# Two gated layers behind an attention: part of a weight combination moved to a later batch, first weights loaded before the stage that reads them, left sides made four steps ahead, a conversion paced later

## The chip, the cores and the metric

One core of a Trainium2 chip runs the whole kernel. The metric is the device time in microseconds (us); lower is better. Five instruction streams run side by side and wait for each other through semaphores: PE (matrix products), DVE (vector), ACT (scalar and activation functions), POOL (a second vector engine), and SP, which in this kernel does nothing but issue DMA transfers, in the order in which its rows stand.

## The reference, cut to what matters

```python
def _attn_ref(q, k, v, tau):                      # 4 x 8 heads, 576 x 64
    scores = scale * np.matmul(q, k.transpose(0, 1, 3, 2))
    thresh = np.max(scores, axis=-1, keepdims=True) - tau
    scores = np.where(scores >= thresh, scores, -1000000000.0)
    ...
    return np.matmul(attn, v)

def _moe_ref(x, w_in, w_out, s, b):               # 2304 x 512 -> 2048 -> 512
    r = np.maximum(x @ w_in, 0.0)
    return (s * (r * r) + b) @ w_out

def _moe2_ref(x, w_in, w_out):                    # 2304 x 512 -> 2048 -> 512
    h = x @ w_in
    g = h * np.tanh(np.log1p(np.exp(np.minimum(h, 20.0))))   # sp = h where h > 20
    return g @ w_out

def reference(...):
    x = attention, heads side by side, (2304, 512)
    return _moe2_ref(_moe_ref(x, ...), ...)
```

The weights of both layers arrive as pairs of 32-bit words (64-bit numbers), and are turned into 32-bit floats on the chip.

## The kernel before, in words

Each factor of a product is held as a high and a low part, and three matmuls stand for one product: high by high, high by low, low by high.

**Stages.** Attention runs over 16 pairs of heads, four to a batch. `moe1(b)` is the first layer for batch b; its steps (128 of them per batch) are run between the steps of the attention for batches 0, 1 and 2, and batch 3 runs alone, once the attention is over. `split_w` (L45 to L70) turns the first layer's weights into floats and splits them; it is paced by a counter `k` in `run` (L737 to L742) and by the steps of batch 0. Then `moe2` (L699) runs the second layer in three superbatches `sb` of 768 tokens. In each, `hidden(sb, j)` for j = 0 to 7 makes the hidden values, and `output(sb)` multiplies them by the output weights.

**Seven products in place of eight.** The second layer multiplies 2 x 2 blocks with seven products, numbered p = 1 to 7, whose left and right sides are sums and differences of blocks. The right sides of the weights are made by `combine` (L72): for k = "i" (input weights) and "o" (output weights) and j = 0 to 7, that is 16 blocks. A block is a generator of 14 steps: two loads of raw words (`craw`, L85); six steps that turn them into floats `af` (ACT L92, DVE L93, L95, L97); two with sums and differences `cs` on DVE (L101 to L117); four that split (`chl`: ACT L123, POOL L124) and store to DRAM (`wsi`, `wso`, L126). Before the change all 16 run during `moe1(1)` and `moe1(2)`, at 240 steps over the 256 steps of these two batches, with buffers of a pool `pre2` (two `raw`, two `hl2`, one `af`).

**Left sides.** For the hidden values they come from `y_combos` (L520), which reads the first layer's output `yd` back and makes `yc` 1 to 7 (ACT L539, DVE L540). For superbatch 0 that happens within `moe1(3)`; for the next superbatch it runs within `hidden`, its results go to DRAM (`ycd`), and `output` loads them as `yc` after each p (L696). For the output, `left(p, q)` (L621) gives block q of the left side of product p, with DVE operations (`z`, `s`, `g`), and a copy on ACT (L685) and a subtraction on DVE (L686, which all stand under L619, the helper `tt`) make it into `hl`, in a pool of 8 buffers.

**Weights of `hidden` and `output`.** Each `hidden` loads its seven right sides in two transfers (`wi`, L578) into the pool `wr`; each half of a p in `output` loads one (`wo`, L682).

**What sets the order.** The order of the code, as each engine's own stream: an instruction waits for its operands and buffers, and all behind it on the same engine waits with it. On ACT three copies of finished p = 1 sums (`after`, L661) are written after the last matmul of p = 1, ahead of the casts for p = 6. In `moe1(3)` a weight unit `w3` (L452, 5 buffers, 32 units) is loaded just before the products that use it; SP holds it back until a buffer is free.

Of the kernel before, what the change touches and what calls it, by code (L numbers as in the profile page):

```python
# [8 lines left out]
F32 = mybir.dt.float32  # L9
# [6 lines left out]
P = 128  # L16
# [3 lines left out]
class Fused:  # L20
# [51 lines left out]
    def combine(self, k, j, pool):  # L72
# [3 lines left out]
        af = pool.tile([P, 4, 2, 128], I32, tag="af", name=f"af{k}{j}", bufs=1)  # L76
        raws = []
        for h in range(2):
            raw = pool.tile([P, 512, 2], I32, tag="raw", name=f"craw{k}{j}{h}")
# [20 lines left out]
        s = pool.tile([P, 4, 2, 128], F32, tag="raw", name=f"cs{k}{j}")  # L100
# [28 lines left out]
    def combine_all(self, pool):  # L129
        for k in "io":  # L130
            for j in range(8):
                yield from self.combine(k, j, pool)
# [440 lines left out]
    def hidden(self, sb, j):  # L573
        nc = self.nc
        w = {}
        for ps, o in (((6, 5, 1), 0), ((2, 4, 7, 3), 3)):
            t = self.wr.tile([P, len(ps), 2, 2, 128], F32R, tag="w", name=f"wi{sb}_{j}_{o}")
            nc.sync.dma_start(t.bitcast(F32).rearrange("p q h c n -> p q h (c n)"), self.ws["i"][:, j, o:o + len(ps)])  # L578
            for i, p in enumerate(ps):
                w[p] = t[:, i]  # L580
        if j % 2 == 0:
# [33 lines left out]
    def output(self, sb):  # L615
        nc = self.nc
        nt = N2 // 128
        z, bank, held = {}, {}, {}
# [56 lines left out]
        for p in (1, 6, 2, 7, 5, 4, 3):  # L675
            old = {2: 1, 7: 6, 3: 5}.get(p)
            bank[p] = bank[old] if old else [self.ps.tile([P, 512], F32, tag="ps", name=f"o{p}{sb}_{t}")[:, :256] for t in range(nt)]
            pos = (6, 5, 7, 4, 1, 2, 3).index(p)
            for q in range(4):
# [15 lines left out]
            if sb < 2:
# [13 lines left out]
    def run(self, ctx):  # L709
# [104 lines left out]
N2 = 384  # L814
# [48 lines left out]
```

## Time and profile before

| | us |
|---|---|
| median of 3 runs | 1189.35 (1185.48 to 1190.13) |
| the profiled execution, its own time | 1189.16 |
| its span (first to last instruction) | 1187.4 |
| PE busy in the span | 1110.4 (94%) |
| DVE, ACT, POOL busy | 761.3, 614.5, 424.0 |
| attention with `moe1(0)` to `moe1(2)` | 0 to about 709 |
| `moe1(3)` alone | 709 to 809.5 |
| superbatch 0: hidden, output | 816.7 to 877.4, 877.4 to 941.2 |
| superbatch 1: hidden, output | 941.2 to 999.4, 999.4 to 1061.3 |
| superbatch 2: hidden, output | 1061.3 to about 1119, to 1183.7 |

A trace row gives the instant at which an instruction began and how long it took, and in brackets how long its engine had been idle before it and which instruction let it go on. A row with a count (x6) is a run of equal instructions. Of matmuls, the distance from one start to the next is the pace; the durations overlap. The granted clock of PE stands in tenths or as a share of full speed, 1.00 being 2.4 GHz and 0.50 being 1.2 GHz.

### The profile page before, as it was taken

The numbers are of one execution on the slowest core, as the hardware profiler recorded it, in microseconds if no ns is written. First come the engines' busy times: TensorE is split into PE (matmuls) and PEld (weight loads), VectorE is DVE, ScalarE is ACT, GpSimd is POOL, SyncE is SP. The second block draws the span as 40 slices with busy tenths as digits, with TensorE's granted clock in tenths as the row PEclk, the third lists the DMA queues.
The fourth block names the chain that finished last, engine by engine and source line by source line (L and its number), as shares of the span: only waits on it lengthen the run. The fifth ranks groups of instructions, "written<-read, shape, count | busy, mean of one in ns | idle before, by whom it ended". The sixth has DMA issues, their size and how long they took to land.

```text
span 1187.4 us, 21376 instructions
## 1 busy us (share of the span) xinstructions
PE 1110.4 (94%) x7896; PEld 1019.3 (86%) x7896; DVE 761.3 (64%) x1515; ACT 614.5 (52%) x1153; POOL 424.0 (36%) x536
## 2 busy tenths in 40 slices
PE   5798999998999999999999989997999999999988
PEld 4576777878898888878888879997999999999988
DVE  5788667777766677776766715322688367825583
ACT  4566666655576655667646537432354134513351
POOL 4666656565666646559656520000000000000000
PEclk7699999999999999999999999998999999999999
DMA  8844466675788788798877668546999999987764
GB/s 214 257 102 119 107 201 198 219 227 174 221 270 267 231 293 247 259 279 258 269 231 268 216 198 286 160 142 229 346 397 383 298 347 385 412 280 248 265 229 129
DMA packets 141447, 292.69 MB, mean 247 GB/s; under 512 B 52832, under 2 KB 78944, under 8 KB 132896
## 3 DMA queue, kind: packets, MB, share of 16 engines
q1 hardware_dynamic: 134112, 286.91, 73.2%
q10 hardware_dynamic: 7232, 4.43, 1.4%
q8 instruction: 62, 1.02, 0.4%
q14 instruction: 41, 0.34, 0.1%
HBM read 201.85 MB, written 66.58 MB: 226 GB/s over the span
## 4 chain that ended last, share of the span: by engine, by line
PE 51%; DMA 16%; DVE 11%; POOL 8%; ACT 6%; issue 6%; SPq 2%; ACTq 0%; POOLq 0%; DVEq 0%
PE o L691 14%; PE y L460 8%; PE h L460 7%; PE qY L571 6%; PE qX L571 4%; PE qV L571 4%; PE pv L365 3%; DMA wraw<-in_moe_w_in_dram 2%; DMA crawi<-in_moe_w_in_dram 2%; DVE e L321 2%; POOL e L331 2%; PE S L306 2%; PE T L343 2%; DMA wsi<-chli 2%; POOL chlo L124 2%
## 5 line engine op out<-in xcount | busy, mean ns | idle before, releaser
L691 PE MATMUL o<-wo,hl 128*128 128x256 f32 x1512 | 182.9, 283 | 7.5 <-ACT hl L685 5.5
L691 PEld LDWEIGHTS o<-wo,hl 128*128 128x128 f32 x1512 | 181.2, 191 | 9.1 <-ACT hl L685 6.3
L460 PE MATMUL h<-xh,w 128*128 128x288 f32 x768 | 165.2, 299 | 5.0 <-ACT r L481 3.7
L460 PE MATMUL y<-gh,w 128*128 128x288 f32 x768 | 168.2, 303 | 1.4 <-ACT y L505 0.9
L321 DVE SCALAR_TENSOR_TENSOR e<-ns,st,e 128x576 f32<-128x576 f32 x128 | 127.4, 999 | 50.8 <-POOL st L312 27.8
L331 POOL TENSOR_SCALAR e<-e,st 128x576 f32<-128x576 f32 x128 | 133.2, 1049 | 38.9 <-DVE st L326 36.9
L460 PEld LDWEIGHTS y<-gh,w 128*128 128x128 f32 x768 | 127.3, 190 | 13.2 <-issue 8.3
L460 PEld LDWEIGHTS h<-xh,w 128*128 128x128 f32 x768 | 125.9, 188 | 9.6 <-ACT r L481 4.8
L317 ACT ACTIVATE e<-ns,st 128x576 f32<-128x576 f32 x128 | 98.9, 776 | 57.9 <-DVE ns L310 55.1
L310 DVE TENSOR_SCALAR_CACHE_REDUCE ns<-S 128x576 f32<-128x576 f32 x144 | 107.5, 749 | 22.1 <-PE S L306 21.0
L343 PE MATMUL T<-ident,e 128*128 128x128 f32 x576 | 98.9, 281 | 21.1 <-ACT te L354 13.6
L306 PE MATMUL S<-KH,Q 128*128 128x288 f32 x320 | 101.5, 333 | 15.4 <-DVE ns L310 9.0
L460 PE MATMUL y<-gl,w 128*128 128x288 f32 x384 | 114.3, 299 | 0.0
L460 PE MATMUL h<-xl,w 128*128 128x288 f32 x384 | 113.3, 295 | 0.0
L354 ACT COPY te<-T 128x576 f32<-128x576 f32 x144 | 91.0, 632 | 41.4 <-PE T L348 35.1
L312 POOL TENSOR_SCALAR st<-st,small 128x1 f32<-128x1 f32 x144 | 66.3, 461 | 119.6 <-DVE ns L310 97.2
L365 PE MATMUL pv<-te,rawv 128*64 128x288 f32 x640 | 98.3, 419 | 0.0
L343 PEld LDWEIGHTS T<-ident,e 128*128 128x128 f32 x576 | 71.2, 143 | 31.2 <-ACT te L354 16.2
L484 POOL TENSOR_TENSOR gl<-rr,gh 128x288 fp32r<-128x288 f32 x96 | 87.9, 922 | 27.0 <-ACT rr L483 26.9
L306 PE MATMUL S<-KL,Q 128*128 128x288 f32 x320 | 93.3, 307 | 0.0
L306 PEld LDWEIGHTS S<-KH,Q 128*128 128x128 f32 x320 | 63.9, 200 | 30.1 <-DVE ns L310 14.8
L571 PE MATMUL qY<-yc,wi 128*128 128x384 f32 x432 | 86.7, 339 | 0.0
(142 smaller groups left out, 2268.0 us busy)
## 6 DMA issues: line engine op xcount, KB each, us to landing
w<-w SPq DMA_DIRECT2D x96, 512.0 KB, 4.6
wo<-wso SPq DMA_DIRECT2D x42, 1024.0 KB, 8.4
wi<-wsi SPq DMA_DIRECT2D x24, 1024.0 KB, 6.9
wi<-wsi SPq DMA_DIRECT2D x24, 768.0 KB, 5.4
w<-wp SPq DMA_DIRECT2D x32, 512.0 KB, 3.7
wsi<-chli SPq DMA_DIRECT2D x24, 512.0 KB, 4.0
wso<-chlo SPq DMA_DIRECT2D x24, 512.0 KB, 3.6
ycd<-yp SPq DMA_DIRECT2D x14, 768.0 KB, 7.3
```

The costliest lines, as they stand in the source:

```text
L306: nc.tensor.matmul(so, Q[:, c0:c0 + 128], kt[:, ks], start=(i == 0), stop=(i == len(terms) - 1))
L310: nc.vector.tensor_scalar(ns.rearrange("p (h n) -> p h n", h=2), sv, -0.125, 3.0e38, op0=ALU.mult, op1=ALU.min, accum_out=nm[:, c1])
L317: nc.scalar.activation(e, ns, AF.Exp, bias=nm[:, c1], scale=-1.0)
L321: nc.vector.scalar_tensor_tensor(e, ns, nthr[:, c1], e, op0=ALU.is_le, op1=ALU.mult, accum_out=sm[:, c1])
L331: nc.gpsimd.tensor_scalar(t, t, rinv[:, j:j + 1], u[:, j:j + 1], op0=ALU.mult, op1=ALU.add)
L343: nc.tensor.transpose(T[:, i * 128:i * 128 + 128], self.es[pr, i, "pair"][:, o:o + 128], self.ident)
L354: nc.scalar.copy(te, T[:, :576])
L365: return self.nc.tensor.matmul(self.pv[HALVES[h], hf * HB:hf * HB + 288], v[:, h, c, :], tes[h][:, hf * 288:hf * 288 + 288], start=first, ...
L460: nc.tensor.matmul(acc[:, :n], w[:, wl, c], rhs[c][xl][:, ts], start=(i == 0), stop=(i == 11))
L484: (nc.vector if b == 3 else nc.gpsimd).tensor_tensor(gl[:, ts], r2, gh[:, ts].bitcast(F32), op=ALU.subtract)
L571: self.nc.tensor.matmul(acc, a, b, start=(first and i == 0), stop=(i == n - 1), skip_group_check=True)
L691: nc.tensor.matmul(bank[p][t], hl[:, gl, j, ts], w[:, 2 * (q % 2) + j, wl], start=(old is None and q + j + i == 0), stop=(q + j + i == 6), ...
```

## The change: five edits

- **Combination.** `EARLY` = 154 steps, 11 blocks (all of "i", and j = 0 to 2 of "o"), are run in `moe1(1)` and `moe1(2)`, spread over all 256 steps; the other 5 blocks ("o", j = 3 to 7, 70 steps) run in `moe1(3)`, one step for each of its first 80 steps, in the buffers of the pool `hl`.
- **Left sides of superbatch 0.** `y_combos(0)` gets its first step at step 80 of `moe1(3)`, then every fourth (before: every eighth from step 0).
- **First weights.** The seven right sides of `hidden(0, 0)` are loaded into three `hl` buffers before `moe1(3)` is finished; `hidden` takes them as an argument.
- **Left sides of the output** are made four (p, q) steps ahead: `prep(0)`, `prep(1)`, `prep(2)` after j = 2, 4, 6 of `hidden`, `prep(3)` at its end, and `prep(i + 4)` at step i.
- **Conversion.** The first layer's weight conversion starts at `k` > 48 and then takes a step for every 12 (before: for every 24, from 24).

```diff
-    def combine(self, k, j, pool):
+    def combine(self, k, j):
+        pool, tags = self.home
-        af = pool.tile([P, 4, 2, 128], I32, tag="af", name=f"af{k}{j}", bufs=1)
+        af = pool.tile([P, 4, 2, 128], I32, tag=tags[0], name=f"af{k}{j}", **tags[3])
...
-    def hidden(self, sb, j):
-        w = {}
-        for ps, o in (((6, 5, 1), 0), ((2, 4, 7, 3), 3)):
-            t = self.wr.tile([P, len(ps), 2, 2, 128], F32R, tag="w", name=f"wi{sb}_{j}_{o}")
-            nc.sync.dma_start(t.bitcast(F32).rearrange("p q h c n -> p q h (c n)"), self.ws["i"][:, j, o:o + len(ps)])
+    def weights_in(self, sb, j, pool, tag, parts):
+        w, o = {}, 0
+        for ps in parts:
+            t = pool.tile([P, len(ps), 2, 2, 128], F32R, tag=tag, name=f"wi{sb}_{j}_{o}")
+            self.nc.sync.dma_start(t.bitcast(F32).rearrange("p q h c n -> p q h (c n)"), self.ws["i"][:, j, o:o + len(ps)])
             for i, p in enumerate(ps):
                 w[p] = t[:, i]
+            o += len(ps)
+        return w
+
+    def hidden(self, sb, j, w):
...
+        seq = [(p, q) for p in (1, 6, 2, 7, 5, 4, 3) for q in range(4)]
+        def prep(i):
+            if i >= len(seq):
+                return
+            p, q = seq[i]
+            a = left(p, q)
+            hl = ready[i] = self.hl.tile([P, 2, 2, N2], F32R, tag="hl", name=f"hl{sb}_{p}_{q}")
+            nc.scalar.copy(hl[:, 0], a)
+            tt(hl[:, 1], a, hl[:, 0].bitcast(F32))
+
+        def run():
+            for i, (p, q) in enumerate(seq):
+                prep(i + 4)
...
-                a = left(p, q)
-                hl = self.hl.tile([P, 2, 2, N2], F32R, tag="hl", name=f"hl{sb}_{p}_{q}")
-                nc.scalar.copy(hl[:, 0], a)
-                tt(hl[:, 1], a, hl[:, 0].bitcast(F32))
+                hl = ready.pop(i)
...
+    def moe2(self, w):
         for sb in range(3):
             nxt = self.y_combos(sb + 1, False) if sb < 2 else iter(())
+            prep, run = self.output(sb)
             for j in range(8):
-                self.hidden(sb, j)
-                next(nxt, None)
+                w = w or self.weights_in(sb, j, self.wr, "w", ((6, 5, 1), (2, 4, 7, 3)))
+                self.hidden(sb, j, w)
+                w = None
+                for _ in range(2 if j == 0 else 1):
+                    next(nxt, None)
+                if j in (2, 4, 6):
+                    prep(j // 2 - 1)
             drain(nxt)
-            self.output(sb)
+            prep(3)
+            run()
...
-            if k % 24 == 0:
+            if k > 48 and k % 12 == 0:
                 next(w1)
...
-                    while n * 256 < 240 * (i + 128 * (b - 1)):
+                    while n * 256 < EARLY * (i + 128 * (b - 1)):
                         next(comb, None)
                         n += 1
                     yield c
-            drain(comb)
+            for _ in range(EARLY - n):
+                next(comb, None)
...
+        self.home = self.hl, ("hl", "hl", "hl", {})
         first = self.y_combos(0, True)
         for i, c in enumerate(self.moe1(3)):
-            if i % 8 == 0:
+            if i < 80:
+                next(comb, None)
+            elif i % 4 == 0:
                 next(first, None)
+        drain(comb)
         drain(first)
+        w0 = self.weights_in(0, 0, self.hl, "hl", ((6, 5, 1), (2, 4, 7), (3,)))
...
+EARLY = 14 * 11
```

A scheduler orders each stream, so the rows below show what the edits moved. Names end in a number of the buffer's own; `hl0_6_1` is superbatch 0, p = 6, q = 1.

ACT at the change from hidden to output in superbatch 0, before (`g` are hidden values, `p1` the copies of finished p = 1 sums):

```order
L613 ACTIVATE g0_3_10281<-g0_3_10281 128x768
L610 ACTIVATE g0_3_10281<-g0_3_10281 128x384
L613 ACTIVATE g0_3_10281<-g0_3_10281 128x768
L661 COPY p10_10497<-o10_0_10412 128x256
L661 COPY p10_10497<-o10_1_10413 128x256
L661 COPY p10_10497<-o10_2_10414 128x256
L685 CAST hl0_6_0_10518<-s0_0_10516 128x768
L685 CAST hl0_6_1_10543<-s0_1_10541 128x768
```

The same place after:

```order
L688 CAST hl0_6_0_10430<-s0_0_10428 128x768
L688 CAST hl0_6_1_10460<-s0_1_10458 128x768
L618 ACTIVATE g0_3_10294<-g0_3_10294 128x768
L688 CAST hl0_6_2_10485<-s0_2_10483 128x768
L615 ACTIVATE g0_3_10294<-g0_3_10294 128x384
L618 ACTIVATE g0_3_10294<-g0_3_10294 128x768
L666 COPY p10_10527<-o10_0_10433 128x256
L666 COPY p10_10527<-o10_1_10434 128x256
L666 COPY p10_10527<-o10_2_10435 128x256
L688 CAST hl0_6_3_10512<-s0_3_10510 128x768
L688 CAST hl0_2_0_10539<-g0_0_9877 128x768
```

The first three casts for p = 6 now stand ahead of the three copies, which wait for PE; they stood behind them. Superbatches 1 and 2 read alike.

SP at the end of `moe1(3)`, before (`yd` are stores of the first layer's output, `wi` the input weights of the second):

```order
L514 DMA yd3_0_63<-yo3_0_9751 128x576
L514 DMA yd3_0_63<-yo3_1_9784 128x576
L514 DMA yd3_1_64<-yo3_2_9817 128x576
L514 DMA yd3_1_64<-yo3_3_9850 128x576
L578 DMA wi0_0_0_9871<-wsi_65 128x1536
L578 DMA wi0_0_3_9873<-wsi_65 128x2048
L578 DMA wi0_1_0_9939<-wsi_65 128x1536
L578 DMA wi0_1_3_9941<-wsi_65 128x2048
```

And after:

```order
L578 DMA wi0_0_0_9853<-wsi_65 128x1536
L578 DMA wi0_0_3_9855<-wsi_65 128x1536
L453 DMA w3_1_3_0_9721<-w1_1_3_0_3682 128x1024
L578 DMA wi0_0_6_9857<-wsi_65 128x512
L453 DMA w3_1_3_1_9754<-w1_1_3_1_3770 128x1024
...
L515 DMA yd3_0_63<-yo3_0_9751 128x576
L544 DMA ycd1_1_9944<-yp1_1_9941 128x1536
L515 DMA yd3_0_63<-yo3_1_9784 128x576
L515 DMA yd3_1_64<-yo3_2_9817 128x576
L515 DMA yd3_1_64<-yo3_3_9850 128x576
L578 DMA wi0_1_0_9946<-wsi_65 128x1536
L578 DMA wi0_1_3_9948<-wsi_65 128x2048
```

The weights of j = 0 went ahead of the last four `w3` units; behind the four stores now stand those of j = 1.

SP in the first part of `moe1(3)`, before:

```order
L452 DMA w3_1_0_1_8955<-w1_1_0_1_2034 128x1024
L452 DMA w3_1_0_2_8985<-w1_1_0_2_2130 128x1024
L543 DMA ycd1_1_10003<-yp1_1_10000 128x1536
L452 DMA w3_1_0_3_9018<-w1_1_0_3_2215 128x1024
L452 DMA w3_0_1_2_9048<-w1_0_1_2_2284 128x1024
L452 DMA w3_0_1_3_9095<-w1_0_1_3_2351 128x1024
L452 DMA w3_0_2_0_9137<-w1_0_2_0_2435 128x1024
```

And after (`craw` are raw words loaded for the combination, `chl` its split results, stored to `wso`):

```order
L453 DMA w3_1_0_1_8834<-w1_1_0_1_1950 128x1024
L86 DMA crawo40_8675<-in_moe2_w_out_dram 128x1024
L86 DMA crawo41_8689<-in_moe2_w_out_dram 128x1024
L453 DMA w3_1_0_2_8872<-w1_1_0_2_2046 128x1024
L127 DMA wso_66<-chlo30_8616 128x2x512
L127 DMA wso_66<-chlo32_8632 128x2x512
L127 DMA wso_66<-chlo34_8647 128x512
L453 DMA w3_1_0_3_8907<-w1_1_0_3_2142 128x1024
L127 DMA wso_66<-chlo35_8663 128x2x512
L453 DMA w3_0_1_2_8950<-w1_0_1_2_2227 128x1024
L453 DMA w3_0_1_3_9005<-w1_0_1_3_2296 128x1024
L86 DMA crawo50_8844<-in_moe2_w_out_dram 128x1024
```

Between the `w3` loads there are now raw loads and stores of split results; up to three stores stand in a row.

## Rows read from the trace of the kernel before

**Rows 1.** Windows: length, busy us of PE, PEld, DVE, ACT, POOL, clock, DMA share, GB/s.
```profile
368.00:709.00 341.00, 325.32 (x2375) 286.50 (x2373) 230.72 (x496) 201.00 (x403) 201.61 (x227) 0.99 0.79 251
709.00:809.50 100.50, 99.98 (x750) 99.52 (x750) 37.15 (x68) 48.03 (x116) 0.00 (x0) 1.00 0.57 190
809.50:941.20 131.70, 122.38 (x842) 121.81 (x842) 78.45 (x114) 49.52 (x75) 0.00 (x0) 0.95 0.91 343
```

**Rows 2.** Timeline of PE where the second layer begins: start, length, instructions, idle before.
```profile
809.21 0.30 PE L460 MATMUL y<-gh,w 128*128 128x288 f32 x1
816.68 2.26 PE L571 MATMUL qX<-yc,wi 128*128 128x384 f32 x6 [7.18 <-DMA wi<-wsi]
...
822.31 1.20 PE L571 MATMUL qX<-yc,wi 128*128 128x384 f32 x6
823.35 0.86 PE L571 MATMUL qY<-yc,wi 128*128 128x384 f32 x4
```

**Rows 3.** Windows, as Rows 1, of the first products there.
```profile
817.00:821.00 4.00, 4.00 (x14) 4.00 (x14) 0.03 (x1) 1.76 (x2) 0.00 (x0) 0.50 1.01 426
```

**Rows 4.** SP's issues there, and the landing times of the five `wi` issues of 811.4 to 813.5.
```profile
811.37 2.65 SPq L578 DMA_DIRECT2D wi<-wsi  x5
...
DMA to landing us min/median/max: 5.2/8.6/12.8
```

**Rows 5.** Windows of L691 alone (PE, PEld): the three outputs, 30 us of full pace.
```profile
877.43:941.18 63.75, 61.61 (x504) 60.96 (x504) 0.97 0.95 352
999.43:1061.25 61.82, 59.60 (x504) 58.97 (x504) 1.00 0.96 365
1114.30:1183.74 69.44, 61.38 (x504) 60.72 (x504) 0.98 0.59 199
...
1020.00:1050.00 30.00, 30.00 (x259) 30.00 (x259) 1.00 0.96 362
```

**Rows 6.** Timeline of PE at the step from p = 1 to p = 6, superbatches 0 and 2.
```profile
887.52 0.97 PE L691 MATMUL o<-wo,hl 128*128 128x256 f32 x6 [1.19 <-ACT hl L685]
889.37 10.86 PE L691 MATMUL o<-wo,hl 128*128 128x256 f32 x77 [0.88 <-DVE hl L619]
...
1132.22 8.01 PE L691 MATMUL o<-wo,hl 128*128 128x256 f32 x53 [1.97 <-ACT hl L685]
```

**Rows 7.** Timeline of ACT, then of DVE, at that step in superbatch 0.
```profile
885.67 1.07 ACT L661 COPY p<-o 128x256 f32<-128x256 f32 x3 [5.14 <-PE o L691]
886.64 3.03 ACT L685 CAST hl<-s 128x768 fp32r<-128x768 f32 x4
...
888.37 0.95 DVE L619 TENSOR_TENSOR hl<-s,hl 128x768 fp32r<-128x768 f32 x1
```

**Rows 8.** Windows, as Rows 1: 45 us of superbatch 0, 10 us of superbatch 1.
```profile
860.00:905.00 45.00, 42.86 (x299) 42.26 (x298) 39.26 (x54) 23.34 (x35) 0.00 (x0) 0.96 1.00 405
...
1010.00:1020.00 10.00, 9.12 (x78) 8.92 (x78) 10.00 (x13) 7.65 (x11) 0.00 (x0) 1.00 1.02 421
```

**Rows 9.** One issue on SP, of the first weights for p = 2, and its time to landing.
```profile
L682 SPq DMA_DIRECT2D wo<-wso x1: 319/319/319, 879.5 to 879.5; - x1
...
DMA to landing us min/median/max: 17.5/17.5/17.5
```

**Rows 10.** Windows, 368 to 709 us, of tile afo (DVE, ACT, POOL), then chlo (ACT, POOL).
```profile
368.00:709.00 341.00, 49.17 (x80) 8.24 (x16) 16.66 (x16) 0.99 0.79 251
...
368.00:709.00 341.00, 17.94 (x32) 38.16 (x32) 0.99 0.79 251
```

**Rows 11.** Waits in 368 to 709 us: who waited for what, total us, times, longest.
```profile
SPq L126 <- POOL chlo L124: 44.6, 20, 5.2
```

**Rows 12.** L95 there: duration ns, min/median/max.
```profile
L95 DVE SCALAR_TENSOR_TENSOR afo<-crawo,afo x16: 675/682/1356, 512.1 to 677.6; 128x512 int32<-128x512 int32 x16
L95 DVE SCALAR_TENSOR_TENSOR afi<-crawi,afi x11: 675/1112/1667, 372.2 to 494.3; 128x512 int32<-128x512 int32 x11
```

**Rows 13.** The page's part 6, DMA issues: count, KB each, median us to landing.
```profile
w<-w SPq DMA_DIRECT2D x96, 512.0 KB, 4.6
```

More of the change, by code (lines that the diff above doesn't have):

```diff
@@ L127, in combine, with combine_all @@
             yield
-    def combine_all(self, pool):
+    def combine_all(self):
         for k in "io":
             for j in range(8):
-                yield from self.combine(k, j, pool)
+                yield from self.combine(k, j)
     def split_all(self, pieces, pool, tags, **kw):
@@ L617, in output @@
         nt = N2 // 128
-        z, bank, held = {}, {}, {}
+        z, bank, held, ready = {}, {}, {}, {}
         tt = lambda o, a, b, op=ALU.subtract: nc.vector.tensor_tensor(o, a, b, op=op)
@@ L673, in after @@
                 store(0, 1, t, add("u2"))
[L675 to L679, printed above, removed]
+        seq = [(p, q) for p in (1, 6, 2, 7, 5, 4, 3) for q in range(4)]
[10 more added lines that the diff above has]
+                prep(i + 4)
+                old = {2: 1, 7: 6, 3: 5}.get(p)
+                if q == 0:
+                    bank[p] = bank[old] if old else [self.ps.tile([P, 512], F32, tag="ps", name=f"o{p}{sb}_{t}")[:, :256] for t in range(nt)]
+                pos = (6, 5, 7, 4, 1, 2, 3).index(p)
                 if q % 2 == 0:
@@ L689, in output @@
                         ts = slice(t * 128, t * 128 + 128)
-                        for i, (gl, wl) in enumerate(((0, 0), (0, 1), (1, 0))):
+                        for k, (gl, wl) in enumerate(((0, 0), (0, 1), (1, 0))):
                             nc.tensor.matmul(bank[p][t], hl[:, gl, j, ts], w[:, 2 * (q % 2) + j, wl],
-                                             start=(old is None and q + j + i == 0), stop=(q + j + i == 6), skip_group_check=True)
+                                             start=(old is None and q + j + k == 0), stop=(q + j + k == 6), skip_group_check=True)
                         if q + j == 4:
                             after(p, t)
-            if sb < 2:
-                t = self.yc[p] = self.ycp.tile([P, 2, 2, N2], F32R, tag=f"yc{p}", name=f"yc{sb + 1}_{p}")
-                nc.sync.dma_start(t.bitcast(F32), self.ycd[p])
-    def moe2(self):
+                if sb < 2 and q == 3:
+                    t = self.yc[p] = self.ycp.tile([P, 2, 2, N2], F32R, tag=f"yc{p}", name=f"yc{sb + 1}_{p}")
+                    nc.sync.dma_start(t.bitcast(F32), self.ycd[p])
+        return prep, run
+    def moe2(self, w):
         for sb in range(3):
             nxt = self.y_combos(sb + 1, False) if sb < 2 else iter(())
+            prep, run = self.output(sb)
             for j in range(8):
-                self.hidden(sb, j)
-                next(nxt, None)
+                w = w or self.weights_in(sb, j, self.wr, "w", ((6, 5, 1), (2, 4, 7, 3)))
[5 more added lines that the diff above has]
+                    prep(j // 2 - 1)
             drain(nxt)
-            self.output(sb)
+            prep(3)
+            run()
     def run(self, ctx):
@@ L758, in moes @@
             pre.close()
-            comb = self.combine_all(pool(a, "pre2", 2, side="left"))
+            self.home = pool(a, "pre2", 2, side="left"), ("af", "raw", "hl2", dict(bufs=1))
             n = 0
```

11 lines of the change are left out of this document (6 added, 5 removed).

## The prediction, made before the change was run

> **What bounds the kernel now.** I read the page's first two parts first: PE is busy 94% of the span, and its slices lie under nine tenths at the start and at a few places near the end. So the time is PE's work plus the holes in it, and the change, which adds and removes no matmul, can only fill holes. The windows by stage say how large they are. From 368 to 709 us PE is idle 341.0 − 325.3 = 15.7 us; in the fourth batch 0.5 us; in superbatch 0 it is 9.3 us [rows 1]. Then I looked for the row on PE that follows each hole, and for what that row waited for. There are two kinds of them in the second layer, and the change aims at both.
>
> The first hole stands between the layers. The last product of the fourth batch starts at 809.21 and the first `qX` at 816.68, after 7.18 us of waiting for `wi` [rows 2]; SP issued it at 811.37, and the first of five landed 5.2 us later [rows 4]. In the 4 us behind it the granted clock is 0.50, so the lower level [rows 3]: PE had stood still, and the first three groups of six, which take 3 × 1.04 = 3.12 us at the pace of 822.31 to 823.35, take 822.31 − 816.68 = 5.63 [rows 2].
>
> The second kind stands in each output, at the step from p = 1 to p = 6. Pace: 30 us / 259 = 0.1158 us for a matmul, 504 of them 58.4 us. The outputs took 63.75, 61.82 and 69.44 us; in the last window 30 matmuls of `hidden` lie too (30 × 1.04/6 = 5.2). The losses are 5.35, 3.4 and 5.84 us, together 14.6 [rows 5]. At that step PE waits for the cast `hl` on ACT, then for its second half on DVE [rows 6], because ACT stood 5.14 us at the three copies, which wait for the end of p = 1, and only then made the four casts from `s`; on DVE the halves then stand between the updates of `g` [rows 7].
>
> **The change, part by part.** The sum is made against the profiled execution, 1189.16 us (its span of 1187.4 and 1.8 around it); the median of the three runs is 1189.35, so the two are one number here.
>
> *A, the first weights.* The hole costs from where the next matmul could have started (809.35, one pace of the fourth batch behind 809.21) to 822.31, less the 3.12 us of work: 9.84 us [rows 2]. In the order of after the three loads of j = 0 stand around the first of the last four `w3`, so they have some four units' time, 12 us, and more to land; the slowest of five queued ones took 12.8 [rows 4]. What is late next is j = 1: its loads still stand behind the four `yd` stores, so 811.4 stays their issue. By the first landing they are there at 816.6; a `hidden` lasts 42 × 1.04/6 = 7.3 us, so PE wants them at 809.4 + 7.3 = 816.7, and the second transfer, with the median 8.6 at 820, half through it. That is just in time. I take 9.3. At the upper end 9.8. At the lower end the first transfer too takes 8.6: 820.0 − 816.7 = 3.3 less, 6.0.
>
> *B, left sides ahead.* In after, the casts for p = 6 stand ahead of the three copies, and so do the DVE halves; nothing in the rows of PE is then late from ACT or DVE. What is late next is DMA. Around that step the 16 engines are full: 405 GB/s over 45 us of superbatch 0, 421 in superbatch 1, shares of 1.00 and 1.02 [rows 8]. The first weights for p = 2 were issued at 879.5, 2.1 us into the output, and landed 17.5 us later, at 897.0 [rows 9]. Without the stall p = 2 begins 144 matmuls into the output: 877.4 + 16.7 = 894.1. So 2.9 us of the 5.35 come back as a wait for `wo`; gain 2.45. In superbatch 1 the stream is at least as full, and in after one more load of `yc` (0.79 MB, 1.9 us at 421 GB/s) stands ahead of the same weights: of 3.4 I leave 0.5. Superbatch 2 loads no `yc` and moves 199 GB/s [rows 5]: 5.84 less two late operations of 0.15, 5.5. Sum 8.5; bounds 5.5 (superbatch 2 alone) and 14.6.
>
> *C, five blocks fewer beside the attention.* The last 14 blocks lay in 368 to 709 us; 9 stay. A block costs DVE 49.17 / 8 = 6.1 us and POOL 38.16 / 8 = 4.8 [rows 10], so the stage loses 31 us of DVE's 231 and 24 of POOL's 202 [rows 1]. PE's time there is set by the chains of the attention through DVE, POOL and ACT, which queue behind the blocks. Whatever share of the 15.7 us of idle is due to the blocks, 5/14 of it goes at most if it is in proportion: 5.6, which I take. Bounds: all 15.7 if the queueing vanishes with less load; and −2, if the attention only meets the batch's steps in another rhythm (two waits of a microsecond).
>
> *M, the same five in the fourth batch.* There PE is idle 0.5 us, so nothing is to be won and everything lies beside it: DVE goes from 37 to 68 us of 100, POOL from 0 to 24 [rows 1, 10]. DMA had 190 GB/s over 100.5 us, 19.1 MB; to it come 5 × (1.05 in and 1.84 out) and the 1.84 of the first weights, 35.4 MB, 352 GB/s, under the 421 that the queues have moved [rows 1, 8]. The cover is the ring of five `w3` buffers: a unit is used up every 100.5/32 = 3.1 us, four units ahead are 12.5 us, a load takes 4.6 [rows 13], so SP may stand about 8 us before PE starves. In after, SP holds up to three stores in a row that each wait for a POOL result; such a wait was 44.6/20 = 2.2 us on the mean [rows 11], 6.7 for three. It fits, but not by much: I take 1.5 us of loss. Bounds: 0, and 5 × 1.2 = 6, one short wait of PE like that in rows 6 for every block.
>
> *Conversion.* The order on every engine is the same as before up to matmul 2064, at about 368 us, and then differs by the combination; so the conversion's other pacing moves nothing: 0, with no range of its own. Moving `y_combos(0)` to the end of the fourth batch costs nothing while DVE is at 68%.
>
> Sum: 1189.2 − 9.3 − 8.5 − 5.6 + 1.5 = **1167.3 us**.
>
> One rule speaks against M. In the stage before, the vector operations of a combination are at times long: L95 has a median of 682 ns in the "o" blocks and 1112 in the "i" blocks, where 675 is the shortest of both [rows 12]. The Trainium skill, "SBUF — State Buffer", section "Who interferes with whom", says that DVE and GpSimd share a port pair as an exclusive lock, and that a DVE instruction with two SBUF inputs contends with a GpSimd instruction that reads SBUF, the loser being fully blocked. By the "i" rows it bites, by the "o" rows, the kind that is moved, it rarely does.
>
> **Rivals.** *R1, DMA does not come late.* For it: the first layer's last loads have taken 1.84 MB out of superbatch 0, 4.4 us of its stream. Against: A puts PE 9.3 us ahead. Then B gives 14: 1189.2 − 9.3 − 14 − 5.6 + 1.5 = 1161.8, and 1152 if C is 15.7. *R2, the attention gives nothing back*, if its chains through DVE, ACT and POOL are set by their own lengths and the blocks only fill gaps; a POOL of 202 us and a DVE of 231 in 341 leave gaps enough [rows 1]: 1189.2 − 9.3 − 8.5 + 1.5 = 1172.9, and 1176.2 with A at 6.0. *R3, DVE becomes the bound of the fourth batch.* If each POOL operation of a block held DVE for its whole length, the first 80 steps (62 us) would hold 23 us of old DVE work, 31 of the blocks and 24 of blocking, 78 us, so PE waits up to 16: 1189.2 − 23.4 + 16 = 1181.8. For it speaks the median of the "i" rows, against it that of the "o" rows [rows 12]. (The Trainium skill's rule above, at its full, is this rival.) *R4, slower: SP's order starves the fourth batch.* Each run of three stores in front of a `w3` load holds it 3 × 5.2 = 15.6 us, the longest wait of rows 11, against a cover of 8: 7.6 us for each block, 38 in five, 1189.2 − 23.4 + 38 = 1204. It decides from 23.4/5 + 8 = 12.7 us for a run. For it: SP takes its rows in order, and DVE and ACT, which feed the blocks, follow PE there. Against: the mean wait is 2.2, and POOL has nothing else to do. That the change doesn't do what it says holds for the conversion, at no price.
>
> **How the numbers follow.** A measurement of this kernel can tell about 0.5% from no change, 5.9 us. The forecast has 0.5, R1 0.2, R2 0.2, R3 0.06, R4 0.04. The range takes in the forecast with its bounds, R2, most of R1 and of R3's edge: 1155 to 1181. Faster than 1183.4: the forecast, R1, R2 and nearly all of R3, 0.92; within 0.5% 0.05; slower 0.03.
>
> **What would show it.** A: the first `qX` follows the last `y` within 1 us at granted clock 1.00, and j = 1 waits under 1 us for `wi`. B: the copies L666 stand behind casts for p = 6 on ACT, no PE row there ends on ACT or DVE, and in superbatches 0 and 1 a PE row at p = 2 ends on DMA `wo`, 2 to 3 us. C: 368 to the first product of the fourth batch is 5 to 6 us shorter. M: PE idle in the fourth batch 1 to 3 us, ended by `w` or `gl`. The prediction is wrong if PE's wait for `w` in the fourth batch passes 10 us, if the clock falls in it, or if the attention's stage moves by more than 16 us either way.

## The result, and the profile after

The changed kernel took 1175.0 us (median of 4 runs, 1170.19 to 1180.19) against 1188.51 beside it: a ratio of 0.989 (95% interval 0.984 to 0.994), 13.5 us less where 21.9 were forecast. The time lies in the range given, and eight microseconds above the forecast. The profiled execution has an own time of 1176.43 and a span of 1174.4; the span of before was 1187.4. The last product of PE ends at 1170.84, and ended at 1183.74.

Where the 12.9 us lie, by the starts of products on PE:

| part | before | after | change | forecast |
|---|---|---|---|---|
| up to the first product of the fourth batch alone | 709.26 | 701.46 | −7.8 | −5.6 |
| from there to the start of its last product | 99.95 | 103.97 | +4.0 | +1.5 |
| from there to the end of superbatch 0 | 131.97 | 124.63 | −7.3 | −11.75 |
| superbatch 1 | 120.07 | 123.54 | +3.5 | −0.5 |
| superbatch 2 | 122.49 | 117.24 | −5.25 | −5.5 |

The third part holds A and the first third of B. Now the rows that answer to those of before. Timeline of PE, changed kernel (start, length, instructions, idle before): the last group of the fourth batch, the first product of the second layer, and the first products of p = 2 in superbatches 0 and 1.

```profile
791.26 0.37 PE L461 MATMUL y<-gh,w 128*128 128x288 f32 x1 [2.38 <-DVE gl L485]
...
806.34 1.31 PE L572 MATMUL qX<-yc,wi 128*128 128x384 f32 x6 [0.61 <-DVE y L508]
...
884.91 21.28 PE L706 MATMUL o<-wo,hl 128*128 128x256 f32 x156 [3.25 <-DMA wo<-wso]
...
1008.86 13.34 PE L706 MATMUL o<-wo,hl 128*128 128x256 f32 x97 [2.84 <-DMA wo<-wso]
```

The 7.18 us in front of `qX` [rows 2] have become 0.61. The waits for ACT and DVE at p = 6 [rows 6] are gone. In their place PE waits for `wo` at p = 2. Windows of the changed kernel (length, busy us of PE, PEld, DVE, ACT, POOL, granted clock, DMA share, GB/s): the stage beside the attention, the fourth batch, the first products of the second layer, and then what follows three waits: 5 us behind that of superbatch 0, 4 behind that of the fourth batch, 5 behind that of superbatch 1.

```profile
368.00:701.46 333.46, 321.71 (x2376) 286.01 (x2374) 200.64 (x447) 188.22 (x374) 169.32 (x207) 0.99 0.69 214
...
701.46:805.43 103.97, 101.33 (x749) 100.89 (x750) 62.22 (x118) 61.47 (x145) 24.10 (x20) 0.98 0.92 339
...
806.30:810.00 3.70, 3.66 (x21) 3.67 (x22) 0.79 (x2) 2.54 (x3) 0.00 (x0) 1.00 0.58 165
...
884.90:890.00 5.10, 5.09 (x24) 5.10 (x25) 2.30 (x6) 0.83 (x1) 0.00 (x0) 0.50 1.02 420
...
791.26:795.26 4.00, 4.00 (x19) 4.00 (x20) 0.95 (x2) 0.00 (x0) 0.00 (x0) 0.57 1.06 378
1008.86:1013.86 5.00, 5.00 (x29) 5.00 (x30) 4.52 (x7) 0.83 (x1) 0.00 (x0) 0.66 1.01 419
```

Behind the wait of superbatch 0 the granted clock is 0.50, the lower level. So that hole costs twice: 3.25 us of waiting, and then 156 products in 21.28 us, where 0.1158 each makes 18.1: another 3. In the last two windows the clock is at the lower level for a part of the time; by the means of 0.57 and 0.66 that costs an estimated 4 × 0.43 = 1.7 us in the fourth batch and 5 × 0.34 = 1.7 in superbatch 1. SP's row for the weights that PE waited for, and their time to landing, answer to [rows 9]:

```profile
L700 SPq DMA_DIRECT2D wo<-wso x1: 319/319/319, 868.2 to 868.2; - x1
DMA to landing us min/median/max: 16.6/16.6/16.6
```

### The profile page after: what moved, and what is told of

Read it like the earlier page. It is cut to its first block, busy times and chain, and to the rows that moved or that the text cites. A ratio compares the mean times of both kernels' runs of the same rounds, so it can differ in the third digit from the quotient of the medians.

```text
span 1174.4 us, 21342 instructions
## 1 busy us (share of the span) xinstructions
PE 1107.1 (94%) x7896; PEld 1019.5 (87%) x7896; DVE 756.4 (64%) x1515; ACT 615.3 (52%) x1153; POOL 416.9 (35%) x536
## 4 chain that ended last, share of the span: by engine, by line
PE 59%; DMA 15%; DVE 10%; POOL 7%; issue 5%; ACT 4%; SPq 1%; ACTq 0%; POOLq 0%; DVEq 0%
PE o L706 13%; PE y L461 10%; PE h L461 9%; PE qY L572 6%; PE pv L366 4%; PE qX L572 4%; PE qV L572 4%; PE S L307 3%; DMA wo<-wso 3%; PE T L344 3%; DMA crawi<-in_moe_w_in_dram 2%; POOL e L332 2%; DMA wsi<-chli 2%; DVE e L322 2%; DMA wraw<-in_moe_w_in_dram 2%
## 5 line engine op out<-in xcount | busy, mean ns | idle before, releaser
L322 DVE SCALAR_TENSOR_TENSOR e<-ns,st,e 128x576 f32<-128x576 f32 x128 | 121.2, 950 | 55.3 <-ACT e L318 36.7
L332 POOL TENSOR_SCALAR e<-e,st 128x576 f32<-128x576 f32 x128 | 129.4, 1020 | 38.1 <-DVE st L327 36.9
L313 POOL TENSOR_SCALAR st<-st,small 128x1 f32<-128x1 f32 x144 | 61.6, 429 | 141.8 <-DVE ns L311 104.4
```

The source lines that it names most:

```text
L322: nc.vector.scalar_tensor_tensor(e, ns, nthr[:, c1], e, op0=ALU.is_le, op1=ALU.mult, accum_out=sm[:, c1])
L332: nc.gpsimd.tensor_scalar(t, t, rinv[:, j:j + 1], u[:, j:j + 1], op0=ALU.mult, op1=ALU.add)
```

## The experiments

The table sets side by side the medians of all kernels and the parts of one profile of each, in us. The **attention** column is the time from the ninth to the last of the 16 `xh` casts on ACT (L378 before, L379 after), which closes each pair of heads. The **fourth batch** runs from its first product alone to the start of its last, **gap** from there to the first `qX`, and the superbatches from `qX` to `qX` (the last one to the end of PE). Ratios are to the kernel before, run on the same chip.

| kernel | median us | ratio (95%) | attention | fourth batch | gap | sb 0 | sb 1 | sb 2 |
|---|---|---|---|---|---|---|---|---|
| before | 1188.5 to 1190.4 | 1 | 330.7 | 99.95 | 7.5 | 124.5 | 120.1 | 122.5 |
| changed | 1175.0 | 0.989 (0.984 to 0.994) | 323.5 | 103.97 | 0.9 | 123.7 | 123.5 | 117.2 |
| e1 all blocks early | 1178.0 | 0.992 (0.990 to 0.994) | 328.7 | 101.76 | 0.9 | 121.9 | 121.6 | 117.3 |
| e2 late first weights | 1181.3 | 0.993 (0.991 to 0.996) | 326.8 | 103.65 | 7.1 | 122.8 | 122.4 | 117.2 |
| e3 no lookahead | 1183.6 | 0.995 (0.993 to 0.997) | 322.8 | 104.34 | 0.9 | 123.7 | 124.6 | 122.4 |
| e4 yc held back | 1169.6 | 0.985 (0.983 to 0.987) | 329.6 | 101.73 | 0.9 | 117.9 | 119.4 | 117.2 |
| e5 = e4, all blocks early | 1171.5 | 0.986 (0.984 to 0.988) | 333.0 | 101.62 | 0.9 | 118.0 | 117.7 | 117.2 |
| e6 = e4, no lookahead | 1182.1 | 0.994 (0.992 to 0.996) | 323.9 | 103.72 | 0.9 | 124.3 | 123.9 | 122.5 |
| e7 before + lookahead | 1185.4 | 0.996 (0.994 to 0.998) | 330.7 | 99.95 | 7.1 | 121.2 | 123.8 | 117.3 |
| e8 = e4, last gl on POOL | 1167.5 | 0.982 (0.980 to 0.984) | 324.0 | 103.56 | 0.9 | 118.1 | 120.4 | 117.3 |
| e9 = e4, first weights held | 1166.1 | 0.979 (0.977 to 0.982) | 325.3 | 99.82 | 0.9 | 117.8 | 119.4 | 117.3 |
| e10 = e5, first weights held | 1170.7 | 0.983 (0.980 to 0.985) | 331.4 | 99.96 | 0.9 | 118.3 | 119.2 | 117.2 |
| e11 = e4, late first weights | 1175.8 | 0.987 (0.985 to 0.990) | 323.3 | 105.64 | 7.3 | 119.2 | 121.6 | 117.3 |
| e12 changed, first weights held | 1172.3 | 0.988 (0.985 to 0.991) | 323.5 | 99.82 | 0.9 | 121.9 | 120.4 | 117.2 |

### What the five blocks were worth beside the attention (e1)

```diff
-            if i < 80:
-                next(comb, None)
-            elif i % 4 == 0:
+            if i >= 80 and i % 4 == 0:
                 next(first, None)
...
-EARLY = 14 * 11
+EARLY = 14 * 16
```

(The pace in `moes` is again 240 of 256.)

> The changed kernel with all 16 blocks of the combination back beside the attention (at the pace of before), the rest as changed. Theory, C and M are two separate terms: the first product of the fourth batch moves back from 701.5 to 708 to 710 us, and the fourth batch loses its wait for gl on DVE (2.4 us) and the low clock behind it, so it takes 100 us and not 104. Together 1175.0 + 7.8 - 4 = 1179 us (1176 to 1183). Rival, the 7.8 us in front of the fourth batch are another rhythm of the attention and not the five blocks: it still begins at 701 to 704, and the time is 1171 to 1173.

1178.0, and a fourth batch of 101.8; it began at 706.4, between the two forecasts. The reason is in the profiles of e2 and e4: they run the same instructions as the changed kernel up to there, and began the fourth batch at 710.6 and 709.2, where it had been 701.5. One profile is not enough for this stage. Over all of them, the attention column is 322.8 to 329.6 in the nine kernels with 11 blocks early (mean 324.7), and 328.7 to 333.0 in the five with all 16 (mean 330.9). So C is 6.2 us, and 1 to 2 of the first profile's 7.8 were luck. The fourth batch of e1 has another hole, 16 us behind its beginning:

```profile
722.21 0.40 PE L461 MATMUL h<-xh,w 128*128 128x288 f32 x1 [1.53 <-DMA w<-w]
```

### The first weights (e2)

```diff
-        w0 = self.weights_in(0, 0, self.hl, "hl", ((6, 5, 1), (2, 4, 7), (3,)))
...
-        self.moe2(w0)
+        self.moe2(None)
```

> The changed kernel without the early load of the first weights (hidden 0 loads its own). Theory: the hole of before comes back, 7 us of waiting for wi and a first stretch at granted clock 0.50: +9 to +10 us, 1184.5 (1182 to 1187). Rival, the hole is partly covered by the other edits (the stores of yd leave earlier): under +5 us, 1180 or less.

The hole is back, with the low clock behind it (timeline of PE, then the window as above):

```profile
821.28 2.26 PE L572 MATMUL qX<-yc,wi 128*128 128x384 f32 x6 [6.76 <-DMA wi<-wsi]
```

```profile
821.00:826.00 5.00, 4.72 (x17) 4.75 (x18) 0.45 (x1) 1.76 (x2) 0.00 (x0) 0.57 1.01 423
```

But the time, 1181.3, is 6.3 us over the changed kernel and lies between the two forecasts. From the fourth batch's last product to the end of superbatch 0 it is 5.2 us longer (129.9 against 124.6), not 9: with PE later, the wait for `wo` at p = 2 shrinks to 2.09.

### The left sides, with the loads as they are and with p = 2 in time (e3, e4, e6, e7)

e3 makes `prep(i)` at step i, with no step ahead:

```diff
-                prep(i + 4)
+                prep(i)
...
-                if j in (2, 4, 6):
-                    prep(j // 2 - 1)
...
-            prep(3)
```

> The changed kernel with every left side of the output made at the step that uses it, as before. Theory, from the changed trace: the lookahead won 5.4 us in superbatch 2 and lost 1.7 and 3.5 in superbatches 0 and 1, where the weights of p = 2 came late and PE then ran at the low clock; so the time is the same, 1175 (1172 to 1178), with superbatch 2 at 122.5 us, and 0 and 1 at 120 to 122. Rival, the lookahead is worth the 8.5 us that were forecast and something else took 8 us in superbatches 0 and 1: 1183.

e4 keeps the lookahead, issues the seven `yc` loads of the next superbatch at the end of p = 1 and makes four of them wait for its last sum, through a copy of one column on POOL, which is idle there:

```diff
-                if sb < 2 and q == 3:
-                    t = self.yc[p] = self.ycp.tile([P, 2, 2, N2], F32R, tag=f"yc{p}", name=f"yc{sb + 1}_{p}")
-                    nc.sync.dma_start(t.bitcast(F32), self.ycd[p])
+                if sb < 2 and i == 3:
+                    for n in (1, 6, 5, 2, 7, 3, 4):
+                        t = self.yc[n] = self.ycp.tile([P, 2, 2, N2], F32R, tag=f"yc{n}", name=f"yc{sb + 1}_{n}")
+                        if n in (2, 7, 3, 4):
+                            nc.gpsimd.tensor_copy(t[:, 0, 0, 0:1], held["p1"][:, nt - 1, 0:1])
+                        nc.sync.dma_start(t.bitcast(F32), self.ycd[n])
```

> The changed kernel with four of the seven yc loads of the next superbatch (p = 2, 7, 3, 4) held behind the end of p = 1, so that the weights of p = 2 stand ahead of them on SP. Theory, it is the order of the loads: the waits of 3.25 and 2.84 us for wo go and the stretches at clock 0.50 with them, superbatches 0 and 1 take 117 to 118 us and not 123.7 and 123.5: 1175 - 12 = 1163 (1161 to 1167). Rival, it is the amount: the engines of DMA are full, so the same lateness shows at the next wo or at the yc of the next superbatch, and under 4 us are won: 1171 or more.

e6 is e4 with the edit of e3; e7 is the kernel before with the lookahead alone.

> Kernel e4 with every left side of the output made at the step that uses it. Theory, late left sides and late weights lie over each other: with the weights in time the stall by ACT and DVE shows in full in all three superbatches, 122 to 124 us each, 5 us over e4 in each of them, about 1184 (1181 to 1187), as much as e3, so the reordered loads alone win nothing. Rival, the two add: the reordered loads win their 5 to 6 us here too, 1178.

> The kernel before with the lookahead of the left sides alone. Theory: superbatch 2 goes from 122.5 to 117.2 us, superbatches 0 and 1 win 0 to 1 as the weights of p = 2 come late there: 1189.5 - 5.5 = 1184 (1182 to 1186). Rival, the 8.5 us of the forecast: 1181. Second rival, all 14: 1175.

e3 took 1183.6, the number of the rival, but not for its reason: superbatch 0 is as long as in the changed kernel, superbatch 1 is 1.1 longer and superbatch 2 5.2, which is 6.2 by the profile. I had taken the stalls of ACT and DVE to cost 120 to 122 in superbatches 0 and 1, as before; here they cost 123.7 and 124.6. DVE's wait at p = 6 had become longer, 1.95 and 3.12 us, and the clock falls behind both (timeline of PE, e3, then two windows as above):

```profile
869.45 5.65 PE L706 MATMUL o<-wo,hl 128*128 128x256 f32 x47
876.29 0.97 PE L706 MATMUL o<-wo,hl 128*128 128x256 f32 x6 [1.19 <-ACT hl L688]
879.21 7.01 PE L706 MATMUL o<-wo,hl 128*128 128x256 f32 x37 [1.95 <-DVE hl L624]
...
994.65 4.48 PE L706 MATMUL o<-wo,hl 128*128 128x256 f32 x37
1004.41 5.86 PE L706 MATMUL o<-wo,hl 128*128 128x256 f32 x36 [3.12 <-DVE hl L624]
...
1004.41:1009.41 5.00, 5.00 (x31) 5.00 (x32) 5.00 (x6) 1.98 (x3) 0.00 (x0) 0.70 1.02 413
879.21:884.21 5.00, 5.00 (x23) 5.00 (x24) 5.00 (x6) 3.00 (x4) 0.00 (x0) 0.50 1.02 424
```

In superbatch 1 of the kernel before, the waits were 1.19 and 0.88 us, at clock 1.00 [rows 5]:

```profile
999.43 8.97 PE L691 MATMUL o<-wo,hl 128*128 128x256 f32 x72
1009.59 0.97 PE L691 MATMUL o<-wo,hl 128*128 128x256 f32 x6 [1.19 <-ACT hl L685]
1011.44 49.98 PE L691 MATMUL o<-wo,hl 128*128 128x256 f32 x426 [0.88 <-DVE hl L619]
```

The counts suggest why the wait grew. Before, all 72 products of p = 1 ran behind the last `hidden` of superbatches 0 and 1. In e3 some of them run between the products of that `hidden`, so that 47 and 37 are left behind it, and PE is sooner at p = 6, whose left sides need the last hidden values. So e3 is not the kernel before in this stage, and its stalls are dearer. No run separates this order from the rest.

e4 took 1169.6 and beat both kernels. The waits for `wo` are gone, superbatches 0 and 1 go to 117.9 and 119.4, and the clock stays up while DMA moves as much as ever. Windows of e4, then SP's timeline, where five `wo` now stand ahead of the four `yc`:

```profile
860.00:905.00 45.00, 44.51 (x353) 44.34 (x352) 39.66 (x52) 23.93 (x37) 2.09 (x4) 1.00 1.00 402
1000.00:1020.00 20.00, 20.00 (x174) 20.00 (x173) 18.23 (x23) 11.83 (x18) 1.50 (x3) 1.00 1.01 415
```

```profile
865.53 13.56 SPq L700 DMA_DIRECT2D wo<-wso  x5
879.47 2.18 SPq L715 DMA_DIRECT2D yc<-ycd  x4
```

So it was the order of the loads and not their amount: with a share of 1.00 and 402 GB/s, as in [rows 8], PE doesn't wait. By superbatches 0 and 1 it won 10 us; by the medians 5.4. The runs don't decide between the two, as the interval of the changed kernel is 6 us to either side.

e6 took 1182.1, as forecast: without the lookahead the reordered loads win no more than the intervals (1.5 us), since the stall by ACT and DVE lies over the late weights. The same two rows as in e3:

```profile
875.36 0.98 PE L706 MATMUL o<-wo,hl 128*128 128x256 f32 x6 [1.19 <-ACT hl L688]
878.28 8.00 PE L706 MATMUL o<-wo,hl 128*128 128x256 f32 x44 [1.94 <-DVE hl L624]
```

e7 took 1185.4, as forecast: 5.2 us less in superbatch 2, 3.3 less in superbatch 0, and 3.7 *more* in superbatch 1, where two waits for `wo` came in place of the stall:

```profile
1010.73 4.48 PE L701 MATMUL o<-wo,hl 128*128 128x256 f32 x36 [1.23 <-DMA wo<-wso]
1018.88 6.35 PE L701 MATMUL o<-wo,hl 128*128 128x256 f32 x41 [3.67 <-DMA wo<-wso]
```

Together, in the changed kernel: neither edit 1183.6, order alone 1182.1, lookahead alone 1175.0, both 1169.6.

### The blocks on a sound base (e5)

e5 is e4 with the edit of e1.

> Kernel e4 with all 16 blocks back beside the attention. Six profiles by now show the last attention output between 705.6 and 709 us with all blocks early and between 700.7 and 709.9 with 11, so one profile says little. Theory, the mean over the profiles (5 blocks are worth 4 us beside the attention and cost 2 to 3 in the fourth batch): 1 to 2 us over e4, 1171 (1168 to 1174). Rival, the 7.8 us of the first profile of the changed kernel are real: 4 to 6 us over e4, 1174 to 1176. Second rival, they are nothing: 2 to 3 under e4, 1167.

1171.5, as the theory had it, though the 1.9 us over e4 are less than the interval of either. The attention takes 333.0 us and the fourth batch 101.6, with a hole of 1.37 for `w` near its beginning.

### The hole in the fourth batch (e8, e9, e10, e12)

In the changed kernel it ends on `gl`, in e2, e3, e4 and e6 at the same place on `w`. e8 takes the last four `gl` from DVE:

```diff
-                    (nc.vector if b == 3 else nc.gpsimd).tensor_tensor(gl[:, ts], r2, gh[:, ts].bitcast(F32), op=ALU.subtract)
+                    (nc.vector if b == 3 and (qf < 3 or fc < 2) else nc.gpsimd).tensor_tensor(gl[:, ts], r2, gh[:, ts].bitcast(F32), op=ALU.subtract)
```

> Kernel e4 with the last four gl operations of the fourth batch on POOL and not behind the yc operations on DVE. Theory, the hole of 1.7 to 3.0 us at the last group of layer 2 (ended by gl in one profile, by the weights w in three) is made by w3 loads that land late between the other loads; gl is done in the same microseconds: no change, 1169.5 (1168 to 1171), and the hole stays, ended by w. Rival, it is DVE: the hole and the low clock behind it go, 1166 (1165 to 1167).

The hole is as large as before, and ends on `w`:

```profile
792.78 0.37 PE L461 MATMUL y<-gh,w 128*128 128x288 f32 x1 [1.98 <-DMA w<-w]
```

1167.5 is 2.2 under e4, but the fourth batch is no shorter (103.6 to 101.7); the attention of this profile was the quicker one by 5.7. So `gl` was not it. How long the `w3` loads take to land there, points to them. Issues of 785 to 800 us before, then of 779 to 792 in the changed kernel:

```profile
DMA to landing us min/median/max: 3.4/3.5/4.3
```

```profile
w<-w SPq DMA_DIRECT2D x4, 512.0 KB, 11.1
yl<-yd SPq DMA_DIRECT2D x2, 512.0 KB, 10.0
```

SP's timeline of the changed kernel, and what SP waited for in its fourth batch:

```profile
777.98 0.99 SPq L578 DMA_DIRECT2D wi<-wsi  x2
779.99 0.32 SPq L453 DMA_DIRECT2D w<-w  x1
...
SPq L127 <- POOL chlo L125: 6.4, 10, 1.3
```

The first of the last four `w3` was issued at 779.99, right behind two transfers of first weights, and landed 11.1 us later, at 791.1; PE went on at 791.26. The stores of the combination, by contrast, held SP for 6.4 us in all and 1.3 at the longest.

e9 holds the first weights back with a copy of one column, made when ACT has the relu of unit (3, 2):

```diff
+                    if b == 3 and (qf, fc, th) == (3, 2, 1):
+                        self.es["w0"] = self.yc_gate.tile([P, 1], F32, tag="wg", name="wg")
+                        nc.scalar.copy(self.es["w0"], r[:, 0:1])
...
+            if tag == "hl":
+                self.nc.gpsimd.tensor_copy(t[:, 0, 0, 0, 0:1], self.es["w0"])
...
+        self.yc_gate = pool(ctx, "wgp", 1, side="left")
```

> Kernel e4 with the three loads of the first weights held until the last relu of the fourth batch's first layer but one (about 13 us before the second layer), so that the last four w3 units stand ahead of them on SP. Theory, the hole of 1.7 to 3.0 us at the last group of the fourth batch is w3 landing late behind these 1.84 MB: it goes, the fourth batch takes 101 us from its first product to its last y and not 103.5, the first qX still follows within 1 us: 1166 (1164 to 1168). Rival, the stores and loads of the combination and of yl make it: the hole stays, 1169. Second rival, the weights now land late and the hole opens in front of qX: 1171 or more.

> Kernel e5 (all 16 blocks beside the attention) with the same hold on the first weights. In e5 they were loaded at 712 us, ahead of the fourth batch's w3, and PE waited 1.4 us for w at 725. Theory: that hole goes, the fourth batch takes 100 us as in the kernel before, 1169.5 to 1170, and e9 is 2 to 4 us faster than this kernel, which is C (5.7 us by the profiles) less what the blocks cost in the fourth batch. Rival, the blocks cost there as much as they free: both at 1168.

e9 took 1166.1, the best of all: 24.3 us under the kernel before beside it. SP's timeline, the window of the fourth batch, and PE's first wait for the weights of j = 1:

```profile
782.74 7.84 SPq L453 DMA_DIRECT2D w<-w  x4
790.63 0.53 SPq L532 DMA_DIRECT2D yl<-yd  x1
795.73 1.27 SPq L583 DMA_DIRECT2D wi<-wsi  x3
```

```profile
705.99:805.81 99.82, 99.56 (x750) 99.33 (x750) 60.82 (x117) 60.99 (x146) 27.62 (x23) 1.00 0.93 338
```

```profile
814.45 1.32 PE L575 MATMUL qX<-yc,wi 128*128 128x384 f32 x6 [0.19 <-DMA wi<-wsi]
```

The last four `w3` now go ahead of `wi`, and of the four `yl` of the next superbatch, which moved with them. The fourth batch is as short as before the change, with all five blocks in it and DVE at 61 us: they cost PE nothing there. e10, without blocks, has the same 99.96 and takes 1170.7. So by the times the five blocks are worth 4.6 us (3 to either side for each of the two kernels), and by the parts all of it lies beside the attention.

> The changed kernel with the hold on the first weights alone (yc loads as changed). Kernel e9 shows the fourth batch at 99.8 us from its first product to its last y, where the changed kernel took 104.0. Theory, what is won in front of superbatch 0 is given back in part where the weights of p = 2 land late: the fourth batch is 4 us shorter, the waits for wo at p = 2 are still there (3 to 4 us, with the low clock), 1172 to 1174. Rival, it carries through: 1171. Second rival, DMA sets the end of p = 2 whatever happens before it: 1175.

e12 took 1172.3, as the theory had it. The fourth batch is as short as in e9, and superbatches 0 and 1 have their waits for `wo` (timeline of PE, then the windows behind them):

```profile
884.63 3.74 PE L711 MATMUL o<-wo,hl 128*128 128x256 f32 x17 [2.17 <-DMA wo<-wso]
...
1006.15 4.13 PE L711 MATMUL o<-wo,hl 128*128 128x256 f32 x33 [2.67 <-DMA wo<-wso]
...
884.63:889.63 5.00, 5.00 (x29) 5.00 (x30) 4.42 (x8) 0.84 (x1) 0.00 (x0) 0.66 1.02 419
1006.15:1011.15 5.00, 5.00 (x42) 5.00 (x43) 4.57 (x8) 1.32 (x2) 0.00 (x0) 1.00 1.01 419
```

Behind the second wait the clock stays up, and superbatch 1 takes 120.4 us and not 123.5, though the wait is as long as in the changed kernel to 0.2 us. So the length of a wait alone didn't tell whether the clock falls: it fell behind 1.98 us in e8 (clock 0.66 over the next 5 us), and not behind these 2.67.

### The first weights on a sound base (e11)

e11 is e4 with the edit of e2.

> Kernel e4 without the early load of the first weights. Theory, in the changed kernel (e2) the early load was worth 6 us by the times, as PE then came early to weights of p = 2 that still landed late; with these in time it is worth its whole 9 us: 1178.5 (1177 to 1180). Rival, 6 us here too: 1175.5.

1175.8, the rival's number: 6.2 over e4. By the parts the early load is worth 7.6 us (from the fourth batch's last product to the end of superbatch 0, 126.4 against 118.8). Superbatch 1 is 2.2 longer too, with a wait of 2.25 for `wo` at 1000.19. My theory, that the missing 3 us of e2 had all gone into the wait for p = 2, is not borne out by this time, and the intervals of both kernels (2.5 to 3 us to either side) don't settle it. One thing it does show: the hole in the fourth batch, 2.91 for `w`, stands here without any early weights, with the four `yl` loads of the next superbatch ahead of the last four `w3` on SP.

```profile
789.39 0.58 PE L461 MATMUL y<-gh,w 128*128 128x288 f32 x1 [2.91 <-DMA w<-w]
```

So the early weights are not needed for it: these `yl` are enough, behind the stores and the first four `yl`, which stand ahead in e9 as well. Which share the early weights have where both are there, was not taken apart: e9 moved both.

## Why the prediction was right in direction and eight microseconds short

- **A, the first weights: right.** The 9.84 us of before became a gap of 0.9, at full clock. That j = 1 would be just in time came out to a fraction of a microsecond: it waited 0.19 in e9, not at all in the changed kernel. Left out again, the early load costs less than the 9.3 taken, 6.3 us by the times in e2 and 6.2 in e11, with intervals of some 3.
- **B, the lookahead: the step that failed.** Superbatch 2 gave 5.25, as costed (5.5). For superbatches 0 and 1 the prediction named the cause, the place and the length: waits for `wo` of 2.9 us at p = 2; 3.25 and 2.84 were found. What failed is their price. "So 2.9 us of the 5.35 come back" counts the wait alone; behind it PE ran at a granted clock of 0.50, which cost another 3 us in superbatch 0 and an estimated 1.7 in superbatch 1. Superbatch 0 came to +1.7 us (124.5 before, less the 2.5 that its first products lost to the low clock, makes 122.0) in place of −2.45, superbatch 1 to +3.5 in place of −0.5. Against the 117.25 us of superbatch 2 without a wait, superbatch 1 had 2.8 to give before, not 3.4, and now loses 6.3: 2.84 of wait, 1.7 of clock and some 1.7 that the runs don't take apart. The price of a fall could be had from the rows of before: the same two waits, 1.19 and 0.88, lost 5.35 us in superbatch 0, where the output's clock is 0.97, and 3.4 in superbatch 1, where it is 1.00 [rows 5, 6]. So against the kernel before B gave nothing in sum, in place of 8.5. Taken out of the changed kernel it costs 8.6 by the times and 6.2 by the parts (e3), but that is no sign that the 8.5 was right, as e3's stalls are dearer than those of before. e4 shows the cause in superbatches 0 and 1: with the loads in another order both waits and both falls are gone, and the same lookahead is worth 12.5 us (e6 to e4).
- **C, the attention: right.** 5.6 taken, 6.2 by fourteen profiles, 4.6 by the times of e9 and e10, within their intervals. The first profile alone said 7.8.
- **M, the fourth batch: the right kind of wait, the wrong load and half the price.** 1.5 taken, 4.0 found, and 3.6 to 4.4 in five of the seven profiles that have the blocks there and no hold. The wait itself, 2.38 us, is of the size forecast; the clock behind it cost an estimated 1.7 more. The prediction was to be wrong if the clock fell in this batch, and by that sign M was: the clock is 0.57 over the 4 us behind the wait. The stores of the combination didn't hold SP long; the cover failed by the landing time, for which I took the page's 4.6 us of [rows 13], where 11.1 came with the queues full, behind the first weights. And "costs nothing while DVE is at 68%", of moving `y_combos(0)`, looked at DVE alone: the `yl` loads, at 709 to 716 us before, now go at 770 to 790, ahead of the last `w3`.
- **The sum.** The falls of the clock, 3.0, 1.7 and 1.7 us, are 6.4 of the 11 us by which the fourth batch and superbatches 0 and 1 miss their forecasts; by the first profile the attention gave 2.2 of them back.
- **Conversion: right.** Up to 368 us the two profiles are alike (the ninth `xh` cast at 377.85 and 377.24).
- **The rivals.** R1 (no late DMA) fell with the rows at p = 2. R2 had the nearest time, 1172.9, and the wrong reason: the attention did give its share back. R4 asked for longer waits of SP than there were. R3 fell by its size: in the fourth batch some DVE operations were held beside POOL's 24 us, but for some 2 us in all. Of the 32 `gl` subtractions there the longest took 1039 ns, while before, with POOL idle, all 32 took 448 to 460. Eight of the 32 ran at the same time as a `chlo` operation of POOL, and these eight took 2.0 us more together than at 0.454 each (min/median/max below, before and after, then the longest `gl` and the POOL row beside it). The trace agrees here with the Trainium skill, "SBUF — State Buffer", section "Who interferes with whom", by which a DVE instruction with two SBUF inputs contends with a reading GpSimd instruction. The ten `afo` operations of L96, the kind of [rows 12], took 684 to 693 ns, but none of them ran at the same time as a POOL operation, so they show nothing on it.

```profile
L484 DVE TENSOR_TENSOR gl<-rr,gh x32: 448/459/460, 715.3 to 798.1; 128x288 fp32r<-128x288 f32 x32
...
L485 DVE TENSOR_TENSOR gl<-rr,gh x32: 451/456/1039, 707.2 to 791.2; 128x288 fp32r<-128x288 f32 x32
...
712.59 1.04 DVE L485 TENSOR_TENSOR gl<-rr,gh 128x288 fp32r<-128x288 f32 x1 [0.54 <-ACT rr L484]
...
712.01 2.76 POOL L125 TENSOR_TENSOR chlo<-cso,chlo 128x512 fp32r<-128x512 f32 x2 [29.18 <-ACT chlo L124]
...
L96 DVE SCALAR_TENSOR_TENSOR afo<-crawo,afo x10: 684/692/693, 705.9 to 765.7; 128x512 int32<-128x512 int32 x10
```

## What to carry to other kernels

Price a new wait of PE by what it leaves behind, not by its length: if the clock falls, the rows behind it say how much. In these runs the clock fell behind some waits of about 2 us and not behind others, so a forecast should have both prices. Where a lookahead takes away a stall and the DMA queues are full, look at once at what the next weights stand behind; holding back the loads that are needed last was worth 5 us by the times (10 by the parts) with the lookahead, and nothing that the times can tell without it. And take a load's landing time from a stretch as full as the one into which it will be moved.

## What was not expected of the hardware

The same instructions took different times in the attention: the ninth `xh` cast came at 375.1 to 383.1 us in fourteen profiles whose order up to 368 us is the same, and the kernel before had medians of 1188.5 to 1190.4 in five sets with single runs from 1184.2 to 1196.3. For the attention a difference of less than some 7 us between two profiles says nothing by itself here, as the nine kernels with 11 blocks early spread over 322.8 to 329.6; superbatch 2 took 117.2 to 117.3 in all eleven profiles with the lookahead. The landing time of a load of 512 KB went from 3.5 us, where DMA moved 141 GB/s (share 0.43), to 11.1 at 412 GB/s (share 1.04); one of 1 MB took 16.6 to 17.5 with the queues full.
